# Batch 0 of a fused attention and feed-forward kernel: score and value blocks of 128 keys by two heads in place of 64 keys by four heads

## The chip, the cores and the metric

One Trainium2 chip; the program runs on one of its cores. The metric is the device time of one execution in microseconds (us). Lower is better.

## The reference

Attention without softmax over q, k and v of 8 batches, 12 heads, 448 positions and head size 64, and then a feed-forward layer over all 3584 tokens:

```
scores = q @ k^T / 8                      per batch and head, 448 x 448
attn   = max(scores, 0)^2 / 448
a      = attn @ v                         448 x 64 per head
x      = heads of a side by side          3584 x 768
out    = gelu(x @ w_in) @ w_out           768 -> 2048 -> 768, exact gelu
```

Inputs and output are float32. The kernel converts inputs to bfloat16 while they are loaded and sums in float32.

## The kernel before

**Attention.** The 12 heads of a batch are taken in 3 groups g of four heads (G). A group's four heads are a square of two by two, named e and j. A block i holds 64 keys of each of the four heads, and 7 blocks (NK) make the 448 keys. `add_steps` (L788) makes one step for each block, or for two half blocks: TensorE computes the scores of 64 keys by 448 queries for the four heads with four matmuls that each use one 64 by 64 quarter of its array (L806), so that the score tile `ps` of 128 partitions holds head j = 0 in its lower and j = 1 in its upper half. One engine then moves the tile out of PSUM with relu and scale into `a_sq` (ScalarE L823 or VectorE L825), and one squares it (VectorE L835 or ScalarE L833). `add_av` (L868) multiplies the seven squared blocks with v, again in quarters of the array, 28 matmuls (L885) into `pav`, which two copies (L548 on VectorE, L550 on ScalarE) bring to `xT`, the input of the feed-forward layer.

**Batch 0** is handled in halves of 224 queries, two blocks a step, so that the first steps can begin when a part of q is there: `halves(0)` (L1525) lists its blocks, of which the first 7 are those of group 0. The k and v of a group are read so that a partition holds 7 consecutive keys (`kv_view`, L508): 1792 bytes in a row of the input for each partition and pair of heads. Group 0's k and half of its q come in float32 at once through the queues of ScalarE and SyncE (L1545 to L1548, `k32` and `q32`), are cast by VectorE and ScalarE (`early`, L1599), and are turned by TensorE transposes: `add_tk` (L659) puts 64 columns for each block and head pair into `tp` and copies it to `kT`; `add_tq` (L687) does the same for q (`qT`). Everything else of batch 0 and all weights come through GpSimd's queue, which casts on the way. From batch 2 on DMA transposes do the turning.

**Feed-forward.** `add_f1` (L936, `psh`), `add_early` and `add_unit` (`pe`, L1103) and `add_blocks` (`pb`, L1256) compute gelu(x @ w_in) into `h_sb`; `add_group` (L1396, `pso`, L1432) computes rows of the output. These use the whole 128 by 128 array and products of sums of blocks, seven in place of eight. The first of them, `psh`, needs the attention result of one half of batch 0.

**Order.** The work is cut into 1618 operations, numbered in the order in which they are made. The string ORDER (L99) lists them by number in the order in which they are put into the engines' queues, with a letter for the engine: P or Q TensorE (Q: with the other kind of PSUM bank), A ScalarE, D VectorE, G GpSimd, S SyncE, and Z for a filler matmul. Each engine works through its own part of the list strictly in that order and waits where an operand isn't ready. HOMES (L83) says which buffer each user of three sorts of buffers gets: "w" are three pairs of PSUM banks, "f" two single banks, "a" fourteen SBUF buffers. The cost constants above it (L37 to L70) were used when such a list was made; with a full list they no longer choose anything.

The quarter matmuls of a score block, which the change replaces for batch 0:

```
for j in range(2):
    moving = q_rows(b)[r, 2 * g + j, cols(half)]
    nc.tensor.matmul(
        side(ps, e)[64 * j : 64 * j + 64, x * w : x * w + w],
        kT[r, g, i * 128 + 64 * j : i * 128 + 64 * j + 64],
        moving, start=True, stop=True,
    )
```

Of the kernel before, what the change touches and what calls it, by code (L numbers as in the profile page):

```python
# [8 lines left out]
F32 = mybir.dt.float32  # L9
# [9 lines left out]
NK = S // KB  # L19
# [59 lines left out]
K_CUT = 4  # L79
# [5 lines left out]
0120120120120120121201201201212012012012020121201200021210010120121021201012021021021020212110010102  # L85
1021021202102102121202020011022012012201201202021011001112020120201210210212012121122002102112012120
200110101201201221021102
""".replace("\n", ""),
    "f": """
0101001010101010101010101010101010101010101001010101010100101010101010101010101010101010010101001101  # L90
0101010
""".replace("\n", ""),
    "a": """
0123456789abcd3201756ac983a0d742156b938da0c756412b3d978a2041bc3d6589147a2b0c9d8365049721c8d53b6a85bd
3a8b8521749c0d638ba015974d2cacdc3806b4180a6db14273a59cb0476218a6093d70263909d76231c504ab8961dc79b061
32c63d602c20d35b841a79b20cd62906c2bc5834a17d609bc1249d3a865
# [3 lines left out]
A13 A19 D16 G2 Q17 D18 P20 D21 Q14 D15 G3 P22 D23 P42 A43 P45 D46 P39 A40 G4 P32 P24 P36 A37 D33 P96  # L100
Z672 A97 D25 P54 Z1024 A55 D41 D44 D47 G6 P26 D27 G7 Q28 D29 P57 A58 G10 P30 D31 P34 D35 D38 P51 A52
P72 D73 D59 D53 P69 A70 D71 D56 Q114 P60 A61 D62 A115 G5 P48 G121 A49 P66 A67 D68 G8 P87 A88 D50 G9
D74 Q78 A79 D116 P99 A100 P84 D85 P63 Q75 A64 A65 D76 D77 A80 P105 A106 D98 P93 P108 D94 A109 D107
G11 P144 A145 P134 D135 P111 A112 P81 A82 A83 G120 D101 P132 D133 G12 P146 A147 D89 D95 D86 P167
P179 A180 P161 A162 P148 D168 A149 G124 P136 D113 P90 A91 A92 P173 D137 D110 Q164 A165 D174 P102
A103 P117 D104 A118 A119 D169 D253 P176 A177 G125 P138 D139 D175 D163 D181 P170 A171 D178 D172 P245
A246 P185 P194 A186 D187 P200 A195 D196 A201 D166 P249 A250 G123 P150 A151 P191 P197 A198 P188 D189
A192 G129 P142 D143 G122 G128 P140 D141 D190 D199 D255 P203 A204 D205 P182 A202 P215 D216 D193 P209
A210 A183 A184 P251 A252 P247 A248 D254 P221 A222 P212 A213 G127 G126 P206 A207 Q224 A225 G131 P261
P278 D257 P268 D256 D258 D260 D279 D262 D226 D259 G152 A208 G153 Q227 P218 A223 A219 D220 P285 A269  # L110
A286 P264 P281 D265 D282 P263 P280 D211 A228 D229 A217 P273 D283 P270 P287 D271 D274 D288 G243 G130
A214 Q230 D266 P290 D291 A231 A232 D376 P276 A284 P293 A294 A277 A275 P378 P395 P380 P397 D374 D375
D377 D379 P381 D383 A292 A384 A267 D396 D400 P385 P402 A403 A386 P398 A382 A399 D412 D413 D415 P416
P433 A401 A417 A434 P390 P404 D405 A406 P407 D408 P419 A289 D391 D414 P387 P436 D388 P423 P440 A272
D458 A409 A420 G240 G241 S233 P410 P393 D450 D451 A437 P425 A424 P442 D426 A441 D443 A394 A389 A411
P428 S234 Q302 D459 A303 P314 A315 G155 G156 G158 G159 A427 P445 D446 A447 P431 P448 Q308 A309 D429
D453 D454 P317 A449 A318 P418 P435 D438 D421 D460 P462 D456 A432 A392 P464 D457 A422 A439 A463 D465
A444 P320 A321 P311 A312 D319 D452 P305 P466 A467 A306 A430 D455 D310 D304 P468 D469 S236 G239 G242
S235 P329 P341 A342 S238 A330 P335 A336 A307 D461 D313 P470 D471 D316 P472 S237 P368 D494 D322 D331
A369 P362 P338 A339 G154 G157 G160 G244 G295 G296 G297 P474 D475 D337 S477 P326 D495 D496 D473 P323  # L120
A363 D364 A327 D328 D340 A324 P344 A345 D346 P332 A333 A325 P498 A499 P500 P353 D501 D334 D343 S478
A354 D355 P359 P350 A351 A360 D497 D352 P502 D503 P365 A370 A366 P347 A348 A349 P356 D357 D367 A358
A361 P504 D505 P506 S479 P532 A533 P523 D524 D507 P526 A527 P508 G298 P520 D521 D522 P514 A515 G299
G300 P371 P517 A518 P529 A530 P510 D372 D373 D588 D586 D509 D587 D534 P590 P607 A608 A591 D589 P592
D595 D516 P597 P614 A615 D598 P610 P593 D624 A611 A594 P609 D612 P602 P619 A531 P616 A613 A519 D620
D617 A618 A621 D603 P626 P643 A596 D644 P599 D600 S482 S481 A627 S483 A601 P628 P645 D528 D648 A649
D631 A632 P629 A630 P605 P622 A606 D511 D625 D525 P633 P650 D634 A623 P646 P635 S480 P547 Q538 A651
P655 A539 S476 A548 D636 A637 P638 D647 D656 A657 P641 P652 D639 A640 P544 A545 G484 G487 P541 D653
D542 A642 G301 G490 Q535 A536 P556 A557 P574 P658 A659 A575 D678 D676 D677 P680 A681 D558 P553 D537
D554 D549 D540 D679 G485 G486 G488 G489 G491 G492 P565 A566 A546 P568 A569 S661 G666 P682 D683 P684  # L130
A555 D570 D543 A685 P562 A654 A563 P577 A578 A604 S512 S660 S662 P550 D551 D552 P686 P688 P725 P571
A572 A726 P559 P716 A717 D687 D564 D696 P690 D576 D689 A718 D560 D561 D573 D579 D691 D567 P719 D720
P728 A729 S663 G669 G493 P580 A581 A582 P692 D693 P700 P722 S695 S513 S665 G672 D697 G667 G668 P734
A723 D735 D721 D701 P583 A584 A585 P731 P749 D750 P702 D703 P752 A753 P740 D741 P704 A705 P792 A732
D698 P706 D699 P708 P809 D727 D724 P794 P811 D707 D733 D788 D789 D736 P799 P816 A730 A810 D709 P712
A751 D817 P821 D814 D791 D790 D713 A793 D797 P710 A798 P795 A815 D800 D711 P812 A813 P804 D822 A796
D805 P755 A823 Q737 A756 P743 A744 P818 D826 D827 P828 P845 A846 A757 P830 P847 D819 P824 D829 P831
D833 P801 D738 A739 D850 A851 P848 A849 A834 P835 P852 A853 D802 P807 A803 A808 D832 P837 A825 P854
A745 G670 G671 D878 D836 P840 D838 S864 D855 S862 S715 D742 S664 P782 A783 Q764 A765 P857 D858 A859
S863 P843 P860 A861 D880 D766 D841 D879 P882 S714 A844 A806 A856 P933 P773 S694 P746 D747 G673 D748  # L140
A774 A934 G674 S867 G868 P884 A883 D885 D754 A839 P758 P779 D759 D760 D775 P767 D881 P886 A887 A842
A780 A768 D781 D769 P888 D889 P890 D891 A820 D898 D900 P776 A777 A778 P761 A762 P930 P770 A771 D899
D784 A763 P892 A931 D893 P894 D772 P918 A919 D895 S865 G871 G675 G874 P948 D949 G869 G870 S897 P927
A928 D929 P902 P945 D946 P960 A961 P785 A786 S866 P924 A925 A926 D947 P954 D955 P904 D903 D901 D905
P936 A937 D920 D950 P921 P906 D907 G872 G873 G875 P908 D909 P910 A787 D992 D962 D911 D990 D932 P912
D913 A938 A935 P914 S916 S896 S1066 G876 A922 A923 S1067 S1065 S1068 D915 S917 P994 A995 P942 A943
Q966 P939 D967 P957 A958 Q951 P1011 G1070 D991 D993 P997 P1001 S1064 S1069 G1073 G877 G1076 A940
G1071 G1072 G1074 D941 D956 A998 P1018 A1002 A1019 P1003 D1004 P996 P1013 A1012 D999 D1016 A1005
A968 A1000 P1023 P1006 D1007 A1008 P1014 D1015 P1030 P1047 A1048 D1024 P1020 D1028 D1021 P1032 P1049
D1052 A1017 A1031 D1035 A1022 A1036 P1033 P1050 A1051 A1034 D959 D1029 P1009 P1037 P1054 D1055 P1039  # L150
P1056 D1038 D1040 P1026 D1057 P1042 P1059 D1043 D1080 D1060 D1081 A1041 A1027 A952 P1045 P1062 A1046
A1010 A1063 P1084 A1025 D953 P984 P969 A970 A971 A1053 P978 P1086 D1085 D1082 D944 P1088 D1087 P1090
D979 D985 A1044 A1089 A1061 P972 A973 P1138 D1139 A1058 D1091 P963 A964 P1135 D1136 P975 A976 A965
D1102 A974 A977 D986 P1094 D1095 P1092 D1093 D1083 P981 P1126 D1100 D1101 G1075 A982 D983 G1077
G1078 P1144 A1145 P1104 A1127 A980 P1096 D1097 S1099 P1153 D1154 P1159 A1160 D1128 P987 D988 D989
P1123 A1124 P1150 A1151 D1140 D1155 P1106 A1105 D1107 P1129 P1120 A1121 D1122 D1152 P1132 A1130
P1108 D1109 P1198 P1196 P1213 A1133 P1215 P1110 A1214 D1103 P1112 D1218 D1111 D1197 D1113 A1131
A1161 D1201 P1114 P1116 D1192 D1193 D1134 D1195 D1115 D1117 S1119 A1125 A1137 P1162 A1163 P1141
A1142 A1143 P1168 A1169 Q1147 P1199 A1148 D1194 P1216 D1217 A1202 P1203 P1220 A1221 P1156 A1157
A1158 Q1186 D1200 P1205 P1222 D1146 D1204 D1206 P1208 D1223 A1164 A1224 P1225 P1232 P1249 A1233  # L160
A1250 D1209 A1210 P1228 A1229 D1226 D1230 D1231 P1234 P1251 D1254 A1219 D1237 P1235 P1252 D1236
A1255 D1253 A1227 A1207 P1211 A1238 A1212 D1187 D1149 P1239 P1256 A1240 A1257 P1241 P1258 D1259
D1242 P1180 A1260 D1181 Q1174 A1243 A1175 P1261 P1244 D1262 A1263 P1247 P1264 D1245 A1265 A1248
# [1607 lines left out]
```

## Time and profile before

| | us |
|---|---|
| median of 3 runs | 359.67 (358.12 to 360.7) |
| the profiled execution | 358.11 |
| its span, first to last instruction | 356.3 |
| TensorE busy (98% of the span) | 348.5 |
| VectorE busy (86%) | 306.0 |
| ScalarE busy (74%) | 262.1 |

The span is what the trace covers; the profiled execution took 1.8 us more than it. A matmul is pipelined and its end is modelled, so TensorE's busy time says little of how fast matmuls follow each other; for that one takes the distance from one start to the next. The chain is followed back from the last instruction to what released each step. In the views "PE" is TensorE, "PEld" its weight loads, "ACT" ScalarE, "DVE" VectorE, "POOL" GpSimd and "SP" SyncE; "x28" is a count of instructions, and "64*64" in a matmul's row is the part of the array that it uses.

### The profile page before, as it was taken

To read this page: it belongs to the slowest core of one execution; us is meant where nothing else is said; L and a number is where in the kernel's file an instruction comes from. 1 tells how busy PE (TensorE), PEld (TensorE's weight loads), DVE (VectorE), ACT (ScalarE), POOL (GpSimd) and SP (SyncE) were. 2 spreads that over 40 slices of the span, in tenths; PEclk is the share of its full clock that TensorE was granted. 3 is DMA by queue.
4 is the path that set the end of the run, shared out by engine and by line. 5 is a ranking of instruction groups with operands and counts; after the bars stand their busy time and mean duration, and the time that the engine had idled before them with its cause. 6 is when DMAs were issued, how large, how long until landed. Compare 5 with 4: busy or idle time off the path is not lost.

```text
span 356.3 us, 9246 instructions
## 1 busy us (share of the span) xinstructions
PE 348.5 (98%) x3853; PEld 250.1 (70%) x3853; DVE 306.0 (86%) x524; ACT 262.1 (74%) x431; POOL 102.9 (29%) x138
## 2 busy tenths in 40 slices
PE   7799999999999999999999999999999999999995
PEld 4577789855599555896557965669669856878663
DVE  3999999999898999789996998879987998769563
ACT  4999978999968995478985689879897896126100
POOL 8565842295183101603714129001000000000000
PEclk9999999999999999999999999999999999999999
DMA  9999999999999726999899979538009001012222
GB/s 174 198 204 203 186 192 176 163 158 161 170 154 179 114 44 116 102 199 118 114 166 137 188 101 122 74 107 139 2 2 182 30 2 46 2 45 90 88 90 88
DMA packets 123465, 43.01 MB, mean 121 GB/s; under 512 B 100896, under 2 KB 120096, under 8 KB 123424
## 3 DMA queue, kind: packets, MB, share of 16 engines
q0 software_dynamic: 84432, 22.47, 66.7%
q1 hardware_dynamic: 38448, 19.50, 26.1%
q8 instruction: 30, 0.49, 0.5%
q10 hardware_dynamic: 544, 0.46, 0.4%
q14 instruction: 11, 0.09, 0.1%
HBM read 45.61 MB, written 11.01 MB: 159 GB/s over the span
## 4 chain that ended last, share of the span: by engine, by line
PE 91%; ACT 6%; DMA 1%; DVE 0%; issue 0%; DVEq 0%; ACTq 0%
PE pso L1432 36%; PE pe L1103 30%; PE ps L806 10%; PE pav L885 9%; ACT a_sq L823 5%; PE pb L1256 5%; PE psh L947 2%; DMA k<-in_k_dram 1%; ACT h_sb L1153 1%; PE tp L667 1%; ACT h_sb L957 1%; DVE nk L548 0%; PE tp L696 0%; ACT p_sb L550 0%; DVE kT L548 0%
## 5 line engine op out<-in xcount | busy, mean ns | idle before, releaser
L823 ACT ACTIVATE a_sq<-ps 128x896 bf16<-128x896 f32 (+2 forms) x145 | 117.3, 879 | 14.3 <-PE ps L806 14.1
L835 DVE TENSOR_TENSOR a_sq<-a_sq 128x896 bf16<-128x896 bf16 (+1 forms) x123 | 71.7, 612 | 1.1 <-ACT a_sq L823 0.8
L1432 PEld LDWEIGHTS <-s_sb 128*128 128x128 bf16 x456 | 42.8, 98 | 31.4 <-issue 3.7
L1103 PEld LDWEIGHTS <-win_sb 128*128 128x128 bf16 x624 | 59.3, 98 | 3.3 <-issue 1.8
L1141 DVE TENSOR_TENSOR part<-pe,part 128x448 f32<-128x448 f32 x78 | 45.6, 618 | 7.9 <-PE pe L1103 5.8
L1153 ACT ACTIVATE h_sb<-part 128x448 bf16<-128x448 f32 x78 | 43.0, 583 | 11.1 <-DVE part L1141 10.8
L806 PE MATMUL ps<-qT,kT 64*64 64x448 bf16 (+1 forms) x756 | 48.5, 337 | 2.2 <-ACT a_sq L823 1.9
L1432 PEld LDWEIGHTS <-h_sb 128*128 128x128 bf16 x336 | 31.7, 98 | 23.5 <-issue 4.9
L1103 PEld LDWEIGHTS <-ws 128*128 128x128 bf16 x468 | 44.3, 98 | 3.0 <-issue 2.7
L588 POOL DMA_DIRECT2D nk<-in_k_dram x36 | 34.8, 968 | 32.1 <-DMA kT<-nk 18.3
L833 ACT ACTIVATE a_sq<-a_sq 128x896 bf16<-128x896 bf16 x46 | 43.3, 970 | 0.3
L825 DVE TENSOR_SCALAR a_sq<-ps 128x896 bf16<-128x896 f32 (+1 forms) x40 | 39.8, 1002 | 3.3 <-PE ps L806 3.1
L1432 PE MATMUL pso<-wout_sb,h_sb 128*128 128x384 bf16 x224 | 41.1, 326 | 0.1
L1432 PE MATMUL pso<-t_sb,s_sb 128*128 128x384 bf16 x224 | 41.1, 326 | 0.0
L1432 PE MATMUL pso<-wout_sb,s_sb 128*128 128x384 bf16 (+2 forms) x232 | 41.1, 321 | 0.0
L885 PE MATMUL pav<-a_sq,v_sb 64*64 64x448 bf16 (+1 forms) x756 | 36.1, 329 | 0.2 <-DVE a_sq L825 0.2
L806 PEld LDWEIGHTS <-kT 64*64 64x64 bf16 x756 | 19.9, 105 | 21.9 <-issue 16.0
L1103 PE MATMUL pe<-t_x,win_sb 128*128 128x224 bf16 x312 | 35.3, 259 | 0.0
L550 ACT COPY part<-pe 128x448 f32<-128x448 f32 x50 | 25.0, 538 | 13.8 <-PE pe L1103 11.3
L1103 PE MATMUL pe<-xT,win_sb 128*128 128x224 bf16 x312 | 34.0, 259 | 0.0
L1103 PE MATMUL pe<-t_x,ws 128*128 128x224 bf16 x312 | 33.5, 259 | 0.0
L506 POOL DMA_DIRECT2D nq<-in_q_dram x36 | 30.1, 839 | 5.8 <-DMA wout_sb<-in_moe_w_out_dram 2.9
(72 smaller groups left out, 401.2 us busy)
## 6 DMA issues: line engine op xcount, KB each, us to landing
out_dram<-osb SPq DMA_DIRECT2D x19, 384.0 KB, 2.7
nq<-in_q_dram POOLq DMA_DIRECT2D x37, 112.0 KB, 6.3
nk<-in_k_dram POOLq DMA_DIRECT2D x36, 112.0 KB, 6.5
v_sb<-in_v_dram POOLq DMA_DIRECT2D x5, 672.0 KB, 7.9
v_sb<-in_v_dram POOLq DMA_DIRECT2D x9, 224.0 KB, 8.3
win_sb<-in_moe_w_in_dram POOLq DMA_DIRECT2D x8, 192.0 KB, 9.2
wout_sb<-in_moe_w_out_dram POOLq DMA_DIRECT2D x4, 384.0 KB, 13.5
wout_sb<-in_moe_w_out_dram POOLq DMA_DIRECT2D x1, 1536.0 KB, 18.2
```

The lines of the kernel that those rows point to most:

```text
L506: nc.gpsimd.dma_start(nq[b][:, g0, :, e], rows)
L588: nc.gpsimd.dma_start(nk[b][:, g0, :, e], rows[:, e].rearrange("p (i d) -> p i d", d=D))
L806: nc.tensor.matmul(side(ps, e)[64 * j : 64 * j + 64, x * w : x * w + w], kT[r, g, i * 128 + 64 * j : i * 128 + 64 * j + 64], moving, start ...
L823: A.activation(to, x, AF.Relu, scale=c_att)
L825: V.tensor_scalar(to, x, c_att, 0.0, op0=mybir.AluOpType.mult, op1=mybir.AluOpType.max,)
L833: A.activation(ar, ar, AF.Square)
L835: V.tensor_mul(ar, ar, ar)
L885: nc.tensor.matmul(side(pav[0], e)[o2 : o2 + 64, :w], vt[b][r, 2 * g + e, bass.ts(i, D)], box["a2"][r, e, o : o + w], start=(i == 0), stop ...
L1103: nc.tensor.matmul(bank[name][:, y, z * HS : z * HS + HS], w[:, k, bass.ts(mm, 128)], right()[:, k], start=first and k == 0 and z == 0, st ...
L1141: V.tensor_add(get(to), ps(name), get(other))
L1153: A.activation(h_ring()[:, m : m + 2, o + half[c].start : o + half[c].stop], src().rearrange("p (x n) -> p x n", x=2), AF.Gelu,)
L1432: nc.tensor.matmul(box[bank][:, n0:n1], left()[:, kf], right()[:, kf, n0:n1], start=bool(need) and kf == 0, stop=kf == K2 - 1, skip_group_ ...
```

## The change

For batch 0 alone (`BIG = (0,)`), the 448 keys of a head are split into 384 (`KM`, three to a partition) and the last 64.

- **Scores.** Blocks 0 to 5 now hold 128 keys of one head j of each pair e: one matmul of 64 rows by 128 columns of the array for each e, two for a half block in place of four. Block 6 holds the last 64 keys of the four heads, in quarters as before.
- **Values.** For the 384 keys, matmuls of 128 rows by 64 columns, 12 for a half; then 4 quarter matmuls for the last 64 keys: 16 in place of 28.
- **Steps.** `halves(0)` pairs the blocks anew: 22 steps as before, two of them with a single half block, as before.
- **Loads.** k and v of a group are read in rows of 768 bytes (three keys) through `load_mains`. The last 64 keys of all heads are read in rows of 256 bytes, two DMAs for each of the two tensors: those of v through GpSimd's queue (`add_rests`, `load_rests`), those of k in float32 through SyncE's queue, behind q, into `k32r`, from where one more VectorE cast takes them to all three groups. Group 0's other k comes in two DMAs of equal size, by j, where it was 4 and 3 blocks before.
- **Order.** ORDER and HOMES are new throughout; the list has 1620 operations. It begins so: `G3 A14 G2 D17 Q18 D21 Q15 D16 A20 P22 D23 P24 D25 A19 P38 A39 P41 D42`. Here A14 is the cast of q, D17 and A20 are the casts of group 0's k by j, D21 is the cast of the last keys, Q18 and P22 are group 0's transposes of k, Q15 those of q, P24 those of group 1's k, A19, D23, D25 and D16 the copies that follow them, P38 is the first score step, A39 its relu. Two modes, "K" and "V", name the new forms of matmul for the list's maker.

```
-K_CUT = 4
+K_CUT = 3
+BIG = (0,)
+KA = 3
+KM = 128 * KA
...
+    def load_mains(to, t, b, g0, g1):
+        rows = t[b, 4 * g0 : 4 * g1, :KM].rearrange("h (p a) d -> p h (a d)", a=KA)
+        nc.gpsimd.dma_start(mains(to, b)[:, 4 * g0 : 4 * g1], rows)
+
+    def load_rests(to, t, b, g0, g1):
+        rows = t[b, 4 * g0 : 4 * g1, KM:].rearrange("(x j) p d -> j p x d", j=2)
+        for j in range(2):
+            nc.gpsimd.dma_start(
+                rests(to, b)[64 * j : 64 * j + 64, 2 * g0 : 2 * g1], rows[j]
+            )
...
+                        if b in BIG and i < 2 * KA:
+                            nc.tensor.matmul(
+                                side(ps, e)[:, x * w : x * w + w],
+                                kT[r, g, i * 128 : i * 128 + 128],
+                                q_rows(b)[r, 2 * g + i // KA, cols(half)],
+                                start=True,
+                                stop=True,
+                            )
+                            continue
...
+            for a in range(KA if b in BIG else 0):
+                for j in range(2):
+                    for e in range(2):
+                        o2 = 64 * (e ^ j)
+                        _, box, o = SQ[blocks[KA * j + a]]
+                        nc.tensor.matmul(
+                            side(pav[0], e)[o2 : o2 + 64, :w],
+                            mains(vt, b)[:, 4 * g + 2 * e + j, bass.ts(a, D)],
+                            box["a2"][:, e, o : o + w],
+                            start=(a == 0),
+                            stop=False,
+                        )
...
-    nc.scalar.dma_start(k32[:, :, first], kv_view(k, 0, 0, 1)[:, :, first])
+    nc.scalar.dma_start(k_first[:, 0], k_rows[:, 0])
     nc.sync.dma_start(q32, q_view(0, 0, 1, 0, HC))
-    nc.scalar.dma_start(k32[:, :, rest], kv_view(k, 0, 0, 1)[:, :, rest])
+    nc.scalar.dma_start(k_first[:, 1], k_rows[:, 1])
+    for j in range(2):
+        nc.sync.dma_start(k32r[64 * j : 64 * j + 64], k_rest[j])
...
+    o = early("DVE", lambda: rests(nk, 0), k32r, 5.7)
+    ld_k[0, 0].append(o)
+    ld_k[0, 1][-1] = ld_k[0, 2][-1] = o
+    add_tk(0, 0, KA, NK)
```

More of the change, by code (lines that the diff above doesn't have):

```diff
@@ L99 @@
 ORDER = """
[L100 to L104, printed above, removed]
@@ L841, in add_steps @@
             d = 0.19 * used / S
-            o1 = sch.add((("PE", d, d + 0.18),), fn_qk, deps, need=("w",), mode="A", bias=bias)
+            big = [i < 2 * KA for b, g, i, half in blocks if b in BIG]
+            d += 0.1 * (len(set(big)) > 1)
+            mode = "K" if any(big) else "A"
+            o1 = sch.add((("PE", d, d + 0.18),), fn_qk, deps, need=("w",), mode=mode, bias=bias)
             d = 0.05 + 2 * used / 1200
@@ L864, in add_steps @@
             for blk in blocks:
-                if blk[2] == NK - 1:
-                    add_av(blk, bias)
+                b, g, _, half = blk
+                whole = [(b, g, i, half) for i in range(NK)]
+                if all(x in SQ for x in whole) and (b, g, half) not in AV:
+                    add_av((b, g, NK - 1, half), bias)
     def add_av(blk, bias):
@@ L886, in fn @@
                             side(pav[0], e)[o2 : o2 + 64, :w],
[L887 removed]
+                            rests(vt, b)[r, 2 * g + e] if last else vt[b][r, 2 * g + e, bass.ts(i, D)],
                             box["a2"][r, e, o : o + w],
```

264 lines of the change are left out of this document (155 added, 109 removed).

## The prediction

> **What bounds the kernel now.** I read the profile's page first: the chain that ended last, by engine.
>
> ```profile
> span 356.3 us, 9246 instructions
> PE 91%; ACT 6%; DMA 1%; DVE 0%; issue 0%; DVEq 0%; ACTq 0%
> ```
>
> TensorE holds nine tenths of the chain, ScalarE 6%. Next, stretches of the span, to see where TensorE isn't the bound (columns: wall time, then PE, PEld, DVE, ACT, POOL busy with counts, clock, DMA share, GB/s).
>
> ```profile
> 5.42:20.06 14.64, 12.28 (x330) 9.12 (x331) 13.32 (x29) 12.88 (x22) 10.69 (x16) 1.00 1.35 199
> 20.06:30.00 9.94, 9.71 (x224) 7.94 (x220) 9.51 (x17) 9.79 (x19) 5.45 (x9) 1.00 1.30 202
> 50.00:330.00 280.00, 279.86 (x2878) 202.21 (x2877) 248.88 (x418) 216.05 (x358) 67.68 (x87) 1.00 0.94 111
> ```
>
> From 50 to 330 us TensorE is never idle (279.86 of 280.00), and from 20 us nearly never. Ahead of 20.06, where the first `psh` matmul stands, it is idle for 2.4 us by busy time and for much more by starts. So the time is the time at which TensorE becomes the bound, plus the work then left to it. The chain in order of time shows how the early part goes, and later pieces show what TensorE pays for its order.
>
> ```profile
> 0.74 3.97 DMA k<-in_k_dram
> 4.73 0.65 DVE nk L548
> 5.42 1.16 PE tp L667 x14
> 6.61 0.36 DVE kT L548
> ...
> 7.32 0.41 PE ps L806 x8
> 7.75 7.89 ACT a_sq L823 x11
> ...
> 98.10 0.38 PE ps L806 x8
> ...
> 136.20 1.41 PE pso L1432 x8
> 137.60 0.50 PE ps L806 x8
> 138.11 1.41 PE pso L1432 x8
> ...
> 145.56 1.30 PE pso L1432 x8
> ```
>
> Up to 7.32 it is load, cast, transpose, copy; at 7.75 the first relu begins, and ScalarE is then the bound for eight microseconds without a gap. Eight `pso` matmuls take 1.30 us, but 1.41 behind another array shape; eight `ps` take 0.38, but 0.50 behind `pso`. Each **change of array shape** costs 0.11 to 0.12 us.
>
> **Term 1: the matmuls themselves, 0.** Starts on TensorE:
>
> ```profile
> 8.72 0.58 PE L806 MATMUL ps<-qT,kT 64*64 64x224 bf16 x16 [0.21 <-ACT a_sq L823]
> 9.10 0.45 PE L1577 MATMUL fill<-zero 64*64 64x512 bf16 x2
> ...
> 10.24 0.58 PE L667 MATMUL tp<-ident,nk 128*64 128x128 bf16 x14
> 10.65 0.36 PE L696 MATMUL tp<-ident,nq 112*64 112x112 bf16 x8
> ...
> 14.17 0.86 PE L885 MATMUL pav<-a_sq,v_sb 64*64 64x224 bf16 x28 [0.20 <-DVE a_sq L825]
> 14.83 1.24 PE L806 MATMUL ps<-qT,kT 64*64 64x224 bf16 x24
> ...
> 20.06 1.32 PE L947 MATMUL psh<-xT,win_sb 128*128 128x224 bf16 x12
> 21.31 0.58 PE L696 MATMUL tp<-ident,nq 112*64 112x112 bf16 x16
> 21.83 0.58 PE L806 MATMUL ps<-qT,kT 64*64 64x224 bf16 x16
> 22.64 0.58 PE L667 MATMUL tp<-ident,nk 128*64 128x128 bf16 x14 [0.23 <-ACT h_sb L957]
> ```
>
> Sixteen quarter matmuls take 0.38 us from start to start (8.72 to 9.10), 28 take 0.66 (14.17 to 14.83): 0.095 for each four, and 224 columns a quarter. A `psh` matmul of 224 columns on the whole array takes 1.25/12 = 0.104 with its change of shape. So four quarters already fill the array. Twelve halves by pairs, 6 x 0.095, and four quarters, 0.095, make 0.66 again; a score step of two blocks stays at 0.19. The change drops 144 of 336 matmuls of batch 0 and no time with them, if two halves run together. For 128 by 64 the transposes show that they do: 14 of 128 columns take 0.41 us, 29 ns each, where 128 columns alone take over half of 0.095. For 64 by 128 no row shows it (second rival).
>
> **Term 2: when the first score step starts, +0.5.** Ahead of P38 stand P22, which needs the cast of the last keys (D21), and P24; D21 also stands ahead of the copy of q's transposes on VectorE (D16). So P38 waits for the last keys of k. When do they land?
>
> ```profile
> q10 hardware_dynamic: 348, 0.32, 67.3%
> q1 hardware_dynamic: 349, 0.17, 42.4%
> ...
> q0 software_dynamic: 371, 0.28, 90.4%
> q1 hardware_dynamic: 375, 0.10, 36.3%
> ...
> q0 software_dynamic: 2332, 0.29, 235.3%
> ...
> q0 software_dynamic: 191, 0.10, 145.1%
> ...
> q10 hardware_dynamic: 186, 0.13, 72.1%
> ```
>
> The first two rows are the DMA queues from 2.75 to 4.1 us: ScalarE's and SyncE's queues share one for one and move 0.49 MB, 363 GB/s, 23 bytes per ns and engine. Rows three and four are 48 to 50 us: GpSimd's queue and SyncE's share one for one too, 371 to 375, though one moves three times the bytes. Rows five and six give GpSimd's cast packets: 128 bytes (82 to 84 us) 2 x 16/2332 = 13.7 ns, 512 bytes (6.0 to 6.5) 0.5 x 16/191 = 42 ns; 384 bytes by the line between them 32 ns. The 768 rows of 256 bytes, 48 for each of 16 engines, start when q is through, near 4.0, and first share with k's second half (16 rows an engine, 33 ns); from 4.3 GpSimd's queue takes every second or third turn. Some 10 rows are done by 4.4, the other 38 go at 32 + 11 = 43 to 45 ns, 1.7 us, and k's rest adds 0.2: 6.3. Landing to use takes about 0.7: in the last row, 4.1 to 4.7, ScalarE's queue moves 0.13 MB in 186 packets, 700 bytes each, so it is at the second k with its 768-byte rows, and the first k is cast at 4.73. D21 starts at **7.0**. Its cast takes 0.5 (384 columns, where the 512 of `nk` take 0.65), 22 transposes at 30 ns 0.7, semaphores 0.1: P38 at 8.3, the first relu 0.43 behind it as now, at t0 = 8.7, where it is 7.75. From both sides: if the last keys were never waited for, the first relu could be 0.5 sooner than now, at 7.2, since the first piece of k has 3 blocks in place of 4 to load, cast, turn and copy (0.74 to 7.32 in the chain); with the rows served last of three queues all along, 9.2. I take 8.7, nearest to the one-for-one rows.
>
> ```profile
> 7.75:14.93 7.18, 7.18 (x9) 1.00 1.38 197
> 27.78 0.59 ACT L550 CAST xT<-pav 128x224 bf16<-128x224 f32 x2
> 28.26 1.00 ACT L823 ACTIVATE a_sq<-ps 128x448 bf16<-128x448 f32 x2
> 29.11 0.98 ACT L550 CAST xT<-pav 128x224 bf16<-128x224 f32 x3
> ...
> 13.03 1.08 DVE L825 TENSOR_SCALAR a_sq<-ps 128x896 bf16<-128x896 f32 x1
> 14.03 3.33 DVE L835 TENSOR_TENSOR a_sq<-a_sq 128x896 bf16<-128x896 bf16 x6
> ```
>
> The first four rows are ScalarE: nine whole relus in 7.18, 0.80 each; a half one (28.26 to 29.11, two) 0.43; a copy of x (27.78 to 28.26, two) 0.24. In the new list the last score step ahead of `psh` (P107) waits for the bank that the relu A102 frees, and up to A102 ScalarE's queue holds 14 whole relus, 2 halves, 3 copies: 11.2 + 0.86 + 0.72 = 12.8. VectorE's queue from D25 to the last copy of x that `psh` needs holds three relus of 1.0, 13 whole squares and copies of 0.54 (six in 3.25) and 10 half ones of 0.30: 13.0. So both engines are full, and neither can take work from the other. So `psh` starts at t0 + 12.8 + 0.12 + 0.19 + 0.11 = t0 + 13.2. It now starts at 20.06, but with two score steps and 30 transposes still behind it that the new list puts ahead (21.31 to 21.83, 21.83 and 22.64 rows: 0.51 + 0.38 + 0.41, 1.3). Level is 21.35, so this term is t0 - 8.15: **+0.5** at 8.7, -1.0 at 7.2, +1.0 at 9.2.
>
> **Term 3: changes of shape.** Counted through both lists (inside a value product too, where halves go over to quarters): ahead of the first `psh` 27 in place of 8, behind it 114 in place of 111. Behind it TensorE is the bound and pays: 3 x 0.11 = **+0.3**. Ahead of it, from P38 on, TensorE has 18 x 0.19 + 0.57 of scores, 2.0 of values, 84 transposes (2.6), 0.95 of fillers and 27 x 0.11 = 3.0 of changes: 12.5 in 13.6 us. That fits, but with little cover left where it had several us, and a matmul that is late holds up ScalarE: **+0.4**, between 0 (all hidden) and +1.1 (the slack that would be eaten).
>
> The Trainium skill, DMA: Bandwidth & Descriptors, Specifications, gives 512 B as the least transfer for full rate and says that smaller ones are read, modified and written. The rows of this case do not show it: 13.7 ns for 128 bytes and 42 for 512 lie on a line with little offset. By that rule the 384-byte packets would cost as much as 512 bytes, 42 ns, the last keys would land 0.4 us later, and the sum would be 361.3 in place of 360.9.
>
> **Term 4: everything else, 0.**
>
> ```profile
> POOL win_sb L523 <- DMA v_sb<-in_v_dram: 1.6, 1, 1.6
> ```
>
> Changes between score and feed-forward shapes are 104 in place of 102, in the three above. Bytes are the same. GpSimd issues two DMAs more, some 0.7 us each, in a stretch in which it waits for room behind earlier DMAs anyway; without that cover `win_sb` would come 1.4 us later. More squares go to ScalarE (60 in place of 46 in all), which is idle a quarter of the time. A new order can add or save waits of a few tenths: -0.5 to +1.0.
>
> Sum: 0 + 0.5 + 0.3 + 0.4 + 0 = +1.2. The profiled execution took 358.11 (span 356.3, 1.8 around it): 359.3. It is at the low end of the runs (median 359.67), so against the median, which is what is compared: **360.9**.
>
> **Rivals.**
> 1. *The last keys are in time.* SyncE's queue gets ahead of GpSimd's, whose first packets came only at 4.1 and slowly. Then t0 = 7.2: -1.0 + 0.3 + 0.2, 359.2. For it: q's queue had the lead in the first rows. Against: the one-for-one rows at 48 to 50 us.
> 2. *Halves of 64 rows by 128 columns don't run together* (slower). Each of 72 matmuls of the 18 paired steps then takes 0.095 alone, a step 0.38: +3.4 us ahead of `psh`. It decides as soon as TensorE's 12.5 us outgrow the 13.6; 15.9 does, by 2.3, and the last cover with it: 360.9 + 2.4 = 363.3. Against it: quarters and 128 by 64 halves do run together. The Trainium skill, TensorE: Matmul & The Clock Gate, LDWEIGHTS, has a load cost columns / 1.2 ns, which is 107 ns for 128 columns and 213 for a pair, and would make it so; by that rule four loads of 64 would need 213 too, and four quarters here take 95.
> 3. *The new list waits later*, for a weight or for batch 1's k: 1.5 to 4 us, 363.5. The rows from 50 to 330 leave no sign of what it would be.
> 4. *It does what the smaller count of matmuls suggests*: over 1% faster. All of 144 matmuls at their 24 ns are 3.5 us, and half of them stand where ScalarE is the bound.
>
> **Chances.** Forecast (0 to +2.5 us) 0.6; first rival 0.22; second 0.08; third 0.06; fourth 0.04. The range that should hold 8 in 10: from 357.7 (first rival, less the 1.5 by which the lowest run lies under the median) to 364.0 (second and third). One per cent, 3.6 us, is about what this kernel's runs can tell from no change: faster 0.05, same 0.85, slower 0.10.
>
> **What would show it.** In the trace after: the last-keys cast on VectorE at 7.0 with a wait for a DMA ahead of it (rival 1: below 5.9); the first relu at 8.7; the first `psh` at 22.3; two 64*128 matmuls starting within a few ns and pairs 95 ns apart (rival 2: each 95 ns apart); ScalarE without gaps from the first relu on; TensorE without gaps from 50 to 330. I would be wrong by much if relus waited for score matmuls in 10 to 20 us, or if a load came late.

## The result and the profile after

| | us | runs |
|---|---|---|
| before | 359.51 (358.12 to 360.7) | 6 |
| after | 364.06 (362.01 to 369.5) | 6 |
| ratio | 1.0101, 95% interval 1.0056 to 1.0146 | |
| profiled execution after (span) | 363.25 (361.2) | |

The medians here and below are of all executions; a ratio leaves out those that took over 1.5% more than the fastest of their kernel, here the one of 369.5 us, without which the median after is 363.99.

The changed kernel is about 1% slower. The forecast of 360.9 is 3.2 us too low; the median lies at the upper end of the range, 0.06 above it, and the ratio at the bound of 1%. The profiled executions differ by 4.9 us in span, and that difference is found by place. First the page of the changed kernel, its span and the chain by engine, then its span in stretches cut at the first relu and at the first `psh` matmul (columns as in the prediction).

```profile
span 361.2 us, 8961 instructions
PE 89%; DVE 7%; DMA 2%; ACT 0%; issue 0%; SPq 0%; DVEq 0%; ACTq 0%
```

```profile
0.00:10.88 10.88, 7.26 (x53) 3.46 (x55) 2.12 (x8) 3.00 (x6) 8.04 (x16) 1.00 1.17 168
10.88:26.46 15.58, 14.93 (x229) 9.03 (x225) 14.02 (x28) 14.06 (x20) 11.51 (x17) 1.00 1.41 198
50.00:330.00 280.00, 279.93 (x2891) 203.31 (x2890) 248.89 (x415) 222.18 (x358) 69.01 (x89) 1.00 0.91 111
```

The same cuts in the kernel before:

```profile
0.00:7.75 7.75, 6.18 (x65) 3.06 (x65) 2.40 (x8) 2.52 (x4) 6.83 (x14) 1.00 0.84 170
7.75:20.06 12.31, 10.12 (x286) 7.25 (x275) 11.75 (x26) 12.31 (x20) 8.36 (x13) 1.00 1.35 199
```

The first relu comes 3.1 us later (10.88 for 7.75). From there to `psh` it takes 15.58 us in place of 12.31; 1.3 of that is work that the new list moved ahead of `psh`, so 2.0 are lost. Behind `psh` stand 334.7 us where, with those 1.3 taken off, there were 334.9: nothing lost. 3.1 + 2.0 - 0.2 = 4.9, the whole of it. From 50 to 330 us TensorE is as full as before. ScalarE's 6% of the chain are gone; VectorE has 7%, behind a head of 2% that is one load.

```profile
2.00 6.78 DMA k<-in_k_dram
```

What follows that load, by start in the timeline of the changed kernel:

```profile
4.75 0.36 DVE L575 CAST nk<-k 128x384 bf16<-128x384 f32 x1 [3.73 <-DMA k<-in_k_dram]
...
8.87 0.36 DVE L575 CAST nk<-k 128x384 bf16<-128x384 f32 x1 [3.76 <-DMA k<-in_k_dram]
...
9.29 1.06 PE L716 MATMUL tp<-ident,nk 128*64 128x128 bf16 x16 [2.28 <-DVE nk L575]
...
10.28 1.30 PE L852 MATMUL ps<-qT,kT 64*128 64x224 bf16 x12
...
10.88 1.73 ACT L879 ACTIVATE a_sq<-ps 128x896 bf16<-128x896 f32 x2 [4.08 <-PE ps L852]
...
11.51 0.77 PE L1663 MATMUL fill<-zero 64*64 64x512 bf16 x2
...
17.34 0.56 PE L852 MATMUL ps<-qT,kT 64*128 64x224 bf16 x8
17.83 0.62 PE L1663 MATMUL fill<-zero 64*64 64x512 bf16 x2
```

The first k is cast at 4.75, as before. The cast of the last keys waits 3.76 us for its DMA and starts at 8.87. TensorE stands idle meanwhile, and when it goes on, it goes on at **half clock**: twelve score matmuls take 1.23 us from start to start (10.28 to 11.51), which is six pairs 0.187 us apart and a change of shape; eight at 17.34 take 0.49, four pairs 0.096 apart and a change of shape. The first clock record in this trace stands at 16.88 us, in the kernel before at 6.42. The clock column says 1.00 for 0 to 10.88 all the same: a stretch ahead of the first record counts as full speed. The spacing of like matmuls tells what the column can't.

How the rows of the last keys came in shows in the DMA queues. In the changed kernel from 5.0 to 5.5, from 5.5 to 6.5 and from 7.5 to 8.4 us:

```profile
q0 software_dynamic: 191, 0.07, 187.1%
q1 hardware_dynamic: 35, 0.01, 13.1%
...
q0 software_dynamic: 254, 0.11, 99.1%
q1 hardware_dynamic: 254, 0.06, 43.9%
...
q0 software_dynamic: 346, 0.17, 141.4%
q1 hardware_dynamic: 16, 0.00, 3.3%
```

GpSimd's queue (q0) and SyncE's (q1) keep no fixed share here. SyncE's rows had one turn in six or seven in the first stretch, one for one in the second, and at the end only 16 rows were left. By the starts of the 768 rows in the trace, nine tenths were under way by 6.8 us, but the last 13 came one at a time, 0.07 us apart, from 7.5 to 8.33, and the cast waits for the last one.

### The profile page after: what moved, and what is told of

Same layout as the page of the kernel before. It is cut to its first block, busy times and chain, and to the rows that moved or that the text cites. A ratio compares the mean times of both kernels' runs of the same rounds, so it can differ in the third digit from the quotient of the medians.

```text
span 361.2 us, 8961 instructions
## 1 busy us (share of the span) xinstructions
PE 353.1 (98%) x3709; PEld 250.9 (69%) x3709; DVE 305.8 (85%) x521; ACT 268.0 (74%) x432; POOL 103.8 (29%) x140
## 4 chain that ended last, share of the span: by engine, by line
PE 89%; DVE 7%; DMA 2%; ACT 0%; issue 0%; SPq 0%; DVEq 0%; ACTq 0%
PE pso L1506 36%; PE pe L1177 29%; PE ps L862 9%; PE pav L959 8%; PE pb L1330 4%; DVE a_sq L891 4%; DMA k<-in_k_dram 2%; DVE a_sq L881 2%; PE ps L852 1%; PE psh L1021 1%; PE tp L716 1%; PE tp L743 0%; DVE kT L575 0%; ACT a_sq L879 0%; DVE qT L575 0%
## 5 line engine op out<-in xcount | busy, mean ns | idle before, releaser
L879 ACT ACTIVATE a_sq<-ps 128x896 bf16<-128x896 f32 (+1 forms) x138 | 113.5, 870 | 14.3 <-PE ps L862 9.1
L891 DVE TENSOR_TENSOR a_sq<-a_sq 128x896 bf16<-128x896 bf16 x109 | 64.1, 616 | 0.5
L889 ACT ACTIVATE a_sq<-a_sq 128x896 bf16<-128x896 bf16 x60 | 56.0, 954 | 0.7 <-DVE a_sq L881 0.4
L881 DVE TENSOR_SCALAR a_sq<-ps 128x896 bf16<-128x896 f32 (+1 forms) x44 | 43.7, 1002 | 3.5 <-PE ps L862 2.7
L862 PE MATMUL ps<-qT,kT 64*64 64x448 bf16 (+1 forms) x612 | 43.2, 355 | 0.3 <-DVE a_sq L881 0.2
L959 PE MATMUL pav<-a_sq,v_sb 64*64 64x448 bf16 (+1 forms) x612 | 33.1, 347 | 0.0
L1540 DVE TENSOR_TENSOR osb<-pso,p_sb 128x384 f32<-128x384 f32 x42 | 23.2, 553 | 10.3 <-PE pso L1506 7.1
```

Of the source, the lines that this page charges most:

```text
L862: nc.tensor.matmul(side(ps, e)[64 * j : 64 * j + 64, x * w : x * w + w], kT[r, g, i * 128 + 64 * j : i * 128 + 64 * j + 64], moving, start ...
L879: A.activation(to, x, AF.Relu, scale=c_att)
L881: V.tensor_scalar(to, x, c_att, 0.0, op0=mybir.AluOpType.mult, op1=mybir.AluOpType.max,)
L889: A.activation(ar, ar, AF.Square)
L891: V.tensor_mul(ar, ar, ar)
L959: nc.tensor.matmul(side(pav[0], e)[o2 : o2 + 64, :w], rests(vt, b)[r, 2 * g + e] if last else vt[b][r, 2 * g + e, bass.ts(i, D)], box["a2" ...
```

## The experiments

Three theories. **A**: all is lost at the start, by the late rows of the last keys and by the late full clock that follows from TensorE's idling. **B**: the new forms and their changes of shape cost more than was counted. **C**: the new list makes something wait later. The twelve kernels came in three lots; the kernel before ran beside each, 359.17, 358.96 and 359.03 us in the median.

### a_nowait: the last keys without their wait

```
-    o = early("DVE", lambda: rests(nk, 0), k32r, 5.7)
+    o = early("DVE", lambda: rests(nk, 0) ..., k_first[:, 0], 5.7)
```

> The changed kernel, but the early cast for the last 64 keys (D21) reads the first piece of k, which is there already, in place of the last keys' rows; those rows are still loaded, and nobody waits for them. It leaves out the last keys of batch 0 (their values are wrong). Theory A (the last keys land late, and TensorE, idle meanwhile, gets its full clock late): the first relu starts at 7.3 to 8.0 us in place of 10.9, the first psh by 22.5 in place of 26.5, the time falls by 3.5 to 5 us to 359 to 360.5. Rival B (the new matmul forms and their 27 changes of shape ahead of psh hold up ScalarE): the first relu comes earlier too, but the stretch from it to the first psh grows from 15.6 to over 17 us, and the time falls by less than 2 us, to over 362.

Measured: 362.05 (360.08 to 363.76), ratio 1.0084 (1.0048 to 1.0120), above the 359 to 360.5 that theory A had forecast. Its timeline of the start:

```profile
8.10 2.25 ACT L879 ACTIVATE a_sq<-ps 128x896 bf16<-128x896 f32 x3 [1.53 <-PE ps L852]
...
21.78 1.32 PE L1021 MATMUL psh<-xT,win_sb 128*128 128x224 bf16 x12
```

The start is repaired: first relu at 8.10, `psh` at 21.78, against a level of 21.35. But only 2.0 of the 4.6 us between the medians came back. The rest is lost in a stretch that was full before, from 70 to 100 us, first before, then a_nowait:

```profile
70.00:100.00 30.00, 29.89 (x304) 16.36 (x303) 28.10 (x48) 28.31 (x42) 17.88 (x24) 1.00 1.50 160
```

```profile
70.00:100.00 30.00, 27.36 (x274) 14.58 (x275) 26.37 (x44) 25.77 (x39) 15.02 (x21) 1.00 1.53 156
```

TensorE loses 2.5 us, and its waits in that stretch are one:

```profile
PE ps L862 <- DMA qT<-nq: 2.6, 1, 2.6
```

A score step of batch 3 waits for a transposed q. In the changed kernel itself nobody waited there: the copy on GpSimd that waits for that q stands at 94.69, the score step at 98.73, late anyhow.

```profile
94.69 0.20 POOL L808 COPY gate<-qT 128x16 bf16<-128x16 bf16 x1 [7.28 <-DMA qT<-nq]
...
98.73 0.76 PE L862 MATMUL ps<-qT,kT 64*64 64x448 bf16 x12
```

So the late start covered a second loss, and B is out for the start: with the last keys repaired and all new forms in place, the stretch from relu to `psh` has its forecast length (13.7 us for 13.6).

### a_spin: the full clock sooner

```
-SPIN = 9
+SPIN = 19
```

> The changed kernel with 19 filler matmuls at the start in place of 9, so that TensorE is busy until about 8 us; the last keys are as late as before. Theory A's second part (half clock from 9.3 to 16.9 us costs about 2 us): matmul pairs of 224 columns are 95 ns apart from the first score step on in place of 187, the stretch from first relu to first psh shrinks from 15.6 to about 13.5 us, the time falls by 2 to 2.6 us to 361.4 to 362. If the clock does not matter, because ScalarE and VectorE set the pace there: less than 0.5 us. Rival B: the stretch stays over 15 us at full clock.

Measured: 362.9 (360.48 to 365.71), ratio 1.0116 (1.0056 to 1.0176). In the profiled execution the last-keys cast stood at 8.09, still late, but the clock was full from 3.91:

```profile
9.48 3.00 ACT L879 ACTIVATE a_sq<-ps 128x896 bf16<-128x896 f32 x4 [1.96 <-PE ps L852]
...
23.10 1.32 PE L1021 MATMUL psh<-xT,win_sb 128*128 128x224 bf16 x12
```

13.6 us from relu to `psh`, against 15.6 with the late clock: the 2.0 us of that stretch are the clock's. The median didn't come down to the forecast 361.4 to 362, though, and the ratio is no lower than the changed kernel's: here too the wait near 97 us stands, 4.1 us long and followed by a spell of half clock, seen in the stretches (TensorE, then its weight loads, and so on; the clock stands third from the end):

```profile
97.00:100.00 3.00, 0.43 (x8) 0.29 (x12) 0.00 (x0) 0.00 (x0) 0.20 (x1) 0.91 1.59 140
100.00:103.00 3.00, 3.00 (x20) 1.18 (x12) 2.04 (x3) 1.73 (x2) 1.20 (x3) 0.52 0.89 172
```

### a_twoq: the last keys over two queues

```
-    for j in range(2):
-        nc.sync.dma_start(k32r[64 * j : 64 * j + 64], k_rest[j])
+    for j, queue in enumerate((nc.sync, nc.scalar)):
+        queue.dma_start(k32r[64 * j : 64 * j + 64], k_rest[j])
```

> The changed kernel with the second of the two DMAs of the last keys issued from ScalarE's queue in place of SyncE's. Theory A: two hardware queues against GpSimd's one take two turns of three, the last keys land about 1 us sooner, first relu near 9.9, time down by 0.8 to 1.5 us. If the DMA engines as a whole are the limit and not the turns, the landing moves by less than 0.3 us and the time stays within 0.5 us.

Measured: 366.97 (365.44 to 368.35), ratio 1.0225 (1.0180 to 1.0271). A miss in time: the cast came a microsecond sooner, as forecast (7.78, first relu at 10.02), but the clock had been full from 3.81 to 7.22 and then fell for 10.24 us, three spells on end:

```profile
7.22:17.46 10.24, 9.04 (x112) 5.58 (x112) 7.66 (x16) 5.94 (x8) 7.89 (x12) 0.50 1.58 189
```

`psh` came at 26.02, only 0.4 us sooner than in the changed kernel, and at 98 us the wait stood again, 3.8 us. This run can't tell how much of its time is the queue and how much the clock that it happened to get.

### b_cold: the kernel before with less warm-up

```
-SPIN = 9
+SPIN = 3
```

> The kernel before with 3 filler matmuls at the start in place of 9, so that TensorE idles from about 2.4 to 5.4 us; nothing else differs. Theory A: the full clock comes 3.4 to 10 us later than the 6.4 of before, and the time rises by 1.5 to 2.5 us, to 361 to 362, with half-speed matmuls meanwhile. If the half clock costs nothing where ScalarE is the bound: within 0.5 us of before.

Measured: 359.69 (358.89 to 361.09), ratio 1.0018 (0.9995 to 1.0041). Full clock from 11.57 us in place of 6.42, `psh` at 21.65 in place of 20.06, and 1.6 us more span in the profiled execution, which the median shows only as 0.5, where 1.5 to 2.5 were forecast. A clock that comes late by 5 us, without a late load, costs the kernel before less than half of what the changed one loses; in the changed kernel it came late by 10.

### What waits at 97 us

SyncE transposes k and q of a batch group by group, and a copy on GpSimd (`gate`) holds back the loads of the next batch until the last group's q is transposed. The order of SyncE's queue for batch 2, with the number of the group, is k0 q0 q1 k1 **q2 k2** in the old list and k0 q0 q1 k1 **k2 q2** in the new one. GpSimd's queue in a_nowait, and then in the kernel before, at the gate and the loads behind it:

```profile
72.92 2.13 POOL L651 DMA_DIRECT2D v_sb<-in_v_dram  x3 [0.28 <-issue]
76.91 0.69 POOL L808 COPY gate<-qT 128x16 bf16<-128x16 bf16 x1 [1.85 <-DMA qT<-nq]
77.54 1.96 POOL L618 DMA_DIRECT2D nk<-in_k_dram  x2
```

```profile
71.12 2.17 POOL L608 DMA_DIRECT2D v_sb<-in_v_dram  x3
73.23 0.47 POOL L761 COPY gate<-qT 128x16 bf16<-128x16 bf16 x1
74.02 1.94 POOL L588 DMA_DIRECT2D nk<-in_k_dram  x2 [0.32 <-issue]
```

Before, the gate opens as soon as the loads of v are issued; in a_nowait it waits 1.85 us more for q2, in a_spin 4.12, and batch 3's loads leave at 77.5 and 79.5 in place of 74.0. From the opening of this gate to the landing of batch 3's first q it is 18.6 to 20.7 us in eleven of the fourteen traces (19.6 in the kernel before, 20.4 in a_nowait), so a gate that opens later delays that q by about as much. The three others are a_twoq with 22.0 and the two that move loads behind this gate (f_slack and f_slack_spin, 23). That gave theory C a form that can be tried in both kernels.

### a_q2first: q2 ahead of k2 in the changed kernel

```
-... S238 ... S239 P343 A344 D345 S240 ...
+... S238 ... S240 P343 A344 D345 S239 ...
```

> Edit: the changed kernel with one pair of SyncE's queue exchanged: for the last group of batch 2 the transpose of q is issued ahead of that of k, as in the kernel before. Nothing else differs. Theory C (the new list puts q behind k there; the gate on GpSimd's queue waits for that q, so batch 3's loads leave 2 to 4 us later, and the transposes of batch 3 are late for a score step near 97 us in those runs that don't happen to be late already): the third gate opens at 72 to 74 us, not at 75.6 to 80; batch 3's first transposed q lands by 93 us, against 94.7; the profiled run itself, which had no wait there, stays at 361 to 363.5, while the median falls by 1 to 2 us to 362 to 363 and the runs lie closer together. Theory A (all of the loss is at the start: late last keys and a late full clock): no change, 364 within 1.

Measured: 362.07 (361.52 to 362.71), ratio 1.0080 (1.0062 to 1.0098). The median fell by 2.0 us and the runs lie closer together, as C said. The intervals of the two ratios overlap, though, so the gain isn't clear of noise, and in the profiled execution the gate opened at 75.90, not by 74 (75.61 in the changed kernel). `psh` stood at 25.04 there, 3.7 us behind the level, so the start is still late.

### a_nowait_q2: both repaired

The edits of a_nowait and a_q2first together.

> Edit: as a_nowait (the cast of batch 0's last keys reads rows that are already there; the last 64 keys of batch 0 are left out of the scores, their rows are still loaded), with the q transpose of batch 2's last group ahead of that of k. a_nowait had its first pair of product rows at 21.78 us, as early as the kernel before, but TensorE then waited 2.64 us for a transposed q at 97 us. Theory C: that wait is gone, and the whole change costs nothing: 358 to 359.5, the kernel before's time within 0.3%. Theory A alone, with the wait at 97 us being DMA traffic that the order doesn't set: 361 to 362.5 as a_nowait.

Measured: 359.94 (358.6 to 363.1), ratio 1.0036 (1.0010 to 1.0061). 2.1 us less than a_nowait, with ratios whose intervals just overlap, and a little short of the forecast: nine of twelve executions took 358.6 to 360.7, and three, the profiled one among them (a wait of 2.2 us for q at 96.7), 362.4 to 363.1. The exchange seems to make the wait rarer or shorter; it doesn't abolish it. The order of q2 and k2 isn't the whole of theory C either. The gate opened at 76.41 here without a wait for q2, because the gate of the group ahead of it had opened at 73.67, where it is 70.31 in the kernel before; why that one is later stays open.

### b_k2first: the reverse in the kernel before

```
-... S238 A330 ... P472 S237 P368 ...
+... S237 A330 ... P472 S238 P368 ...
```

> Edit: the kernel before with the reverse exchange: for the last group of batch 2 the transpose of k is issued ahead of that of q. Theory C: the third gate opens 2 to 4 us later than at 73.2; the score step at 94.1 us had its q at 92.78, 1.3 us ahead, so TensorE now waits 1 to 3 us there: 360.5 to 362.5. Theory A: no change, 359.2 within 0.5.

Measured: 363.86 (359.13 to 368.05), ratio 1.0101 (1.0063 to 1.0139). S237 is k2 and S238 is q2. Two words of the order exchanged, and the kernel before takes as long as the changed one. The profiled execution is the fastest of the eight (359.13); it shows the steps on a small scale, and none of the executions that lost time was traced. In the kernel before, the score step had its q 1.3 us ahead of time:

```profile
92.78 0.42 POOL L761 COPY gate<-qT 128x16 bf16<-128x16 bf16 x1 [7.70 <-DMA qT<-nq]
...
94.10 0.76 PE L806 MATMUL ps<-qT,kT 64*64 64x448 bf16 x12
```

With the exchange the gate ahead of the loads waits, and then the score step:

```profile
74.92 0.20 POOL L761 COPY gate<-qT 128x16 bf16<-128x16 bf16 x1 [0.67 <-DMA qT<-nq]
...
95.09 0.76 PE L806 MATMUL ps<-qT,kT 64*64 64x448 bf16 x12 [0.73 <-DMA qT<-nq]
```

### a_first4: a complete version

The last keys of the first four heads alone are loaded ahead of the first score step, the others later by GpSimd's queue; q2 ahead of k2.

```
-    k_rest = k[0, :, KM:].rearrange("(x j) p d -> j p x d", j=2)
+    k_rest = k[0, :4, KM:].rearrange("(x j) p d -> j p x d", j=2)
...
+                if g0 == 1:
+                    load_rests(nk, k, b, 1, G)
...
-    o = early("DVE", lambda: rests(nk, 0), k32r, 5.7)
+    o = early("DVE", lambda: rests(nk, 0)[:, :2], k32r, 5.7)
```

> Edit: a version that leaves nothing out. From the changed kernel: ahead of the first score step only the last keys of the first four heads are loaded and cast (2 x 128 rows instead of 2 x 384); those of the other eight heads come by GpSimd's queue, straight in bf16, behind the first load of k there; and q ahead of k as in a_q2first. Theory A and C together: the last keys' cast starts by 6.5 us instead of 8.87, full clock by 7 to 11 us, the first pair of product rows at 22 to 23 us, and no wait at 97 us: 359 to 360.5. If the rows are late again although they are a third as many (the turns among the queues set it, not the bytes): the cast at 8 us or later and 361 to 363.

Measured: 359.6 (358.55 to 364.35), ratio 1.0030 (1.0000 to 1.0060), apart from a_q2first's 1.0062 to 1.0098. Timeline:

```profile
6.61 0.23 DVE L575 CAST nk<-k 128x128 bf16<-128x128 f32 x1 [1.30 <-DMA k<-in_k_dram]
...
7.46 0.75 PE L854 MATMUL ps<-qT,kT 64*128 64x224 bf16 x12
8.14 0.47 PE L1665 MATMUL fill<-zero 64*64 64x512 bf16 x2
...
21.63 1.32 PE L1023 MATMUL psh<-xT,win_sb 128*128 128x224 bf16 x12
```

The cast starts at 6.61 with a third of the rows, the twelve score matmuls take 0.68 us (full clock from 6.34), `psh` stands at 21.63. The start is repaired, though in the profiled execution a wait of 0.92 us for batch 3's first q is left, which had been forecast to go, and three of the twelve executions took 363.2 to 364.4. The whole is level with the kernel before to 0.3%.

### f_slack, f_slack_spin, f_spin, b_spin: can either be beaten?

f_slack is a_first4 with two moves on GpSimd's queue, f_slack_spin and f_spin are f_slack and a_first4 with 19 warm-up matmuls, b_spin is the kernel before with 19.

```
-... G160 (k2) A308 G161 (q2) ...   ... G159 G162 (two loads of v) G246 (gate) G297 G298 (k, q of batch 3) ...
+... G161 A308 G160 ...             ... G246 G297 G298 G159 G162 ...
```

> Edit: from a_first4 (nothing left out), two moves on GpSimd's queue: batch 2's last load of q ahead of its last load of k, and two of batch 2's three loads of v behind the first loads of k and q of batch 3. Theory C (what is left of the loss is the wait for batch 3's first transposed q near 95 us, 0.92 us in a_first4's profile and more in some of its executions): batch 3's loads leave 1.4 us or more ahead of 75.1, its first q lands by 94 instead of 95.19, no wait there: 358.6 to 359.4, the runs closer together, none at 363 or above. Against it: the wait is set by traffic among the DMAs and not by when the loads leave, 359.6 as a_first4 with its spread; or the moved loads of v are late for the products of batch 2 at 83 to 98 us: 360.5 or more.

> Edit: f_slack with 19 matmuls on zeros at the start instead of 9, so that the full clock should be there by about 4 us as in a_spin and not at 7 or later. Theory A and C: the first pair of product rows 0.3 to 1 us sooner, and with the slack at 95 us made larger that reaches the end: 357.8 to 359, level with the kernel before or up to 0.3% under it. If the slack doesn't hold, TensorE waits at 95 us for what it gained at the start: as f_slack.

> Edit: a_first4 with 19 matmuls on zeros instead of 9, without the moves of f_slack. Theory C: an earlier start is waited off: the first pair of product rows 0.3 to 1 us sooner than 21.63, the wait near 95 us longer by as much, more executions with it, 359.6 to 361.5, not faster than a_first4. Without C: faster than a_first4 by what the start gains, 358.7 to 359.3.

> Edit: the kernel before with 19 matmuls on zeros instead of 9. It shows what the warm-up alone is worth without the change. Its first score step waited for no clock (full clock from 6.42 us), and its slack for batch 3's first transposed q is 1.3 us. Theory C: the start gains up to 0.8 us and the slack takes it in: 358.2 to 359.2, the kernel before within 0.2%; a loss only if the start gains more than 1.3 us.

| | median | ratio |
|---|---|---|
| f_slack | 362.83 (359.06 to 366.25) | 1.0081 (1.0047 to 1.0115) |
| f_slack_spin | 363.52 (360.55 to 366.43) | 1.0088 (1.0056 to 1.0119) |
| f_spin | 359.76 (358.95 to 363.74) | 1.0003 (0.9972 to 1.0033) |
| b_spin | 360.12 (358.99 to 361.95) | 1.0028 (1.0005 to 1.0051) |

f_slack is a clear miss. Its gate opened no sooner (74.73 for 74.49 in a_first4), and the two loads of v now stand between batch 3's first and second group. DMA queues from 92 to 95 us, f_slack first, then a_first4:

```profile
q0 software_dynamic: 1705, 0.21, 153.5%
q1 hardware_dynamic: 1138, 0.28, 62.9%
```

```profile
q1 hardware_dynamic: 1293, 0.32, 113.9%
q0 software_dynamic: 60, 0.01, 3.8%
```

In a_first4 GpSimd's queue (q0) is all but done by then and the transposes, on q1, have the engines; in f_slack the loads still run, the first q lands at 98.0, and the score step waits 3.3 us. The first loads left at 75.68, no sooner than in a_first4 (75.12), so what an earlier start of them is worth wasn't tested; what made q later here is the second explanation on record, traffic. b_spin and f_spin missed at the other end: the ten added matmuls on zeros stood in the way of the first transposes, which began at 6.87 and 7.50 us in place of 5.42 and 5.36, and `psh` came at 21.11 and 22.64 in place of 20.06 and 21.63. No version is faster than the kernel before; f_spin can't be told from it.

## Why the prediction was right, and where it failed

- **Term 1, matmuls 0: right.** Values at full clock, in the changed kernel:

```profile
30.81 0.77 PE L946 MATMUL pav<-a_sq,v_sb 128*64 128x224 bf16 x12
31.51 0.29 PE L959 MATMUL pav<-a_sq,v_sb 64*64 64x224 bf16 x4
```

Twelve halves take 0.70 us with their change of shape, so pairs 96 ns apart; 144 matmuls fewer bring nothing. Rival 2 is about the other form, the scores of 64 rows by 128 columns: the eight that are shown at 17.34 above start in pairs, 96 ns from pair to pair, so it is out too. The rule that the prediction cites for it from the Trainium skill, TensorE: Matmul & The Clock Gate, LDWEIGHTS, would give 213 ns for such a pair of 128 columns each; the trace has 96.

- **Term 2, first score step +0.5: the step that failed.** The mechanism was the right one: D21, the cast of the last keys, waits for a DMA, and everything behind it with it. Its size was off: 8.87 in place of 7.0, beyond the bound that gave 9.2 for the first relu; that came at 10.88, not 8.7. The sum took one mean rate, one turn for one, from 4.4 us on and had all rows landed at 6.3. One for one did come, from 5.5 to 6.5, but not before (35 to 191), so that nine tenths of the rows were under way only by 6.8; and the last ones trailed until 8.33. Why they trailed the trace doesn't show. It isn't the same each time: with the same load and order of queues the cast started at 8.09 in a_spin and at 7.70 in a_q2first. From the landing on, the working held where the clock was full: relu to `psh` 13.6 to 13.8 us for 13.6; cast to relu 2.0 at half clock for 1.7.
- **What Term 2 lacked.** It counted TensorE's work at full clock throughout. A late load leaves TensorE idle, here for 2.3 us, and half clock stood until 16.88: 2.0 us more between relu and `psh`. That idle time and half clock belong together shows best where the clock had been full before: in a_twoq and a_q2first TensorE waited 1.8 and 2.0 us for that cast, and the clock fell at 7.22 and 9.44. From relu to `psh` it is 15.6 to 16.0 us in these three, 13.6 in a_spin, where TensorE was busy with warm-up for longer and waited only 1.1 us, and the clock stayed full. The chain of consequences is load, idle, clock; only its first link was priced.
- **Term 3, changes of shape: right within what can be seen.** +0.4 ahead of `psh`: 13.7 us in a_nowait for the 13.6 forecast with it. +0.3 behind: with Term 4 it comes to -0.2 in the profiled executions.
- **Term 4, the rest 0, and rival 3.** "The rows from 50 to 330 leave no sign" was an oversight: the row that bears on it is that of the score step at 94.10 and its q at 92.78, 1.3 us of slack, and the order of SyncE's queue in the two lists. In the kernel before, exchanging k2 and q2 alone costs 1% (b_k2first), which is shown. In the changed kernel the exchange took 2.0 us off the median, and 2.1 where the start was repaired, neither clear of noise by the intervals. There the start and the wait partly cover each other, and how much of the 1% belongs to which in a given execution varies; in the profiled execution all of it is the start. Rival 3 had the kind of loss right and gave it 0.06, with other waits in mind.
- **The rivals.** The first (last keys in time) was wrong in fact. Its price wasn't reached either: in a_first4, where they are nearly in time and the order is repaired, the ratio to the kernel before is 1.0030, some 1.1 us over it, where 0.5 us less than the kernel before was forecast.
- **The range.** Its upper end, 364.0, came from rivals 2 and 3, not from Term 2. That the median came out beside it is luck: the profiled execution missed by 2.2 us at the first relu and 2.0 by the clock, gained 0.5 on what was forecast behind `psh`, and these happen to add up to about what the rivals cost.

In medians the four corners are: as made 364.06, order repaired 362.07, last keys repaired 362.05, both 359.94 (a_first4: 359.60); about 2 us each. Of these steps only the one from order repaired to both is clear of noise by the intervals of the ratios, and that barely.

## What to carry to other kernels

A load put at the head of an engine's queue should be as small as what the first step needs: a third of the rows landed in time, all of them did not, and the idle time cost clock on top. After a reorder, look for the gates: a transposed tile that frees the next batch's loads can cost more than the 1.3 us of slack that stood at the score step behind it, and an early loss can hide a later one, so a repair has to be measured with both in place. And a mean share of one queue against another says when most rows are there; whoever waits for the last row needs the spread as well, 6.8 us for nine tenths and 8.33 for the last one here.

## What the hardware showed that was not expected

**The clock falls in spells of 3.41 us, and some 2 us of idle time were enough.** Waits at 97 us of 2.2 (a_nowait_q2), 2.8 (f_slack_spin), 3.3 (f_slack), 3.8 (a_twoq) and 4.1 us (a_spin) were followed by 3.41 us at half clock, 1.7 us of work; waits of 0.7, 0.9, 1.4 and one of 2.6 us (a_nowait) were not. In every trace the changes of clock lie whole multiples of 3.413 us behind the first record, and that explains the 2.6. TensorE's stretches between two such points (wall time, busy time with count, clock, DMA share, GB/s), two in a_nowait, then two in a_nowait_q2:

```profile
92.20:95.62 3.42, 2.43 (x15) 1.00 2.46 145
95.62:99.03 3.41, 1.76 (x19) 1.00 0.93 192
...
94.52:97.93 3.41, 1.22 (x16) 1.00 1.30 150
97.93:101.35 3.42, 3.42 (x26) 0.50 0.82 125
```

In a_nowait the wait lies across a point, with 1.0 us of idle time on one side and 1.65 on the other; in a_nowait_q2 all 2.2 us lie in one stretch, and the next is at half clock. In all fourteen traces the clock fell behind every such stretch at full clock with 1.97 us of idle time or more and behind none with 1.67 or less; of three between these it fell behind one (1.82). The times of one kernel then lie on steps: b_k2first's executions with a mean clock of 1.000 took 359.13 and 359.69, at 0.995 (one spell) 362.12 and 363.28, at 0.991 (two) 364.45. The steps are larger than 1.7 us a spell; the rest may be the waits themselves, but none of these executions with spells was traced. The Trainium skill, TensorE: Matmul & The Clock Gate, What's actually happening, tells of a free-running window of about 3.4 us, with half speed after an idle window and full speed after a busy one. The length agrees with these records. But one busy window did not suffice in the changed kernel: by the profile's busy time TensorE was not idle between 10.06 and 13.47, and full clock came at 16.88.

**The transposed q landed when the loads were out.** Batch 3's first q is issued at 87 to 88 us in a_first4 and in f_slack alike and lands at 95.2 and 98.0; the last packets of GpSimd's loads stand at 92.4 and 95.7. In the thirteen traces in which this q was issued before those loads ended it landed 0.7 to 3.2 us behind their last packet, whenever it had been issued.
